# k transposed by pairs of tokens, C's exponentials by token parity, A in token order, one store per output tile, and a new order table

## The chip, the core and the metric

The kernel runs on one core of a Trainium2 chip. The metric is the time of one execution on the device in microseconds. Before the change it is 270.56 us, the median of three runs (270.55 to 273.65). A difference of 2% is 5.4 us.

The core has a matrix engine (TensorE, PE in the profile; its weight loads are PEld), a vector engine (VectorE, DVE), an activation engine (ScalarE, ACT), GpSimd (POOL) and SyncE (SP), which here only issues transfers. PSUM is the memory that PE writes; eight banks of 512 float32 columns on 128 partitions.

## The reference, cut to what matters

Eight batches, eight heads, 576 tokens of 64 elements. Tokens are averaged in 32 segments of 18 (the landmarks). Three softmax matrices are made, a small pseudo-inverse is iterated six times, and the attention's result goes through a two-layer MLP.

```python
q_lm = q.reshape(B, H, m, S // m, D).mean(axis=3)      # m = 32 landmarks
k_lm = k.reshape(B, H, m, S // m, D).mean(axis=3)
A  = sm(q, k_lm)        # 576 x 32 for each head
Bm = sm(q_lm, k_lm)     # 32 x 32
C  = sm(q_lm, k)        # 32 x 576
for _ in range(6):
    Z = 2 * Z - Z @ Bm @ Z
attn = A @ Z @ C @ v
x = attn.transpose(0, 2, 1, 3).reshape(B * S, H * D)   # 4608 x 512
h = x @ w_in                                           # 512 -> 2048
out = (max(h, 0) ** 2) @ w_out                         # 2048 -> 512
```

## The kernel before

**Layout.** A token of a segment r (0 to 31) is r*18 + t, with t from 0 to 17. The eight heads of a batch are two halves i of four groups g; a partition is g*32 + r. q and k are loaded by half (`kraw`, `qraw`), v in four quarters: block c of v's partitions holds tokens t = 9c to 9c + 8.

**Attention of a batch** (`attention`, L474). `tr` (L538 to 549) transposes q and k on PE, six blocks of 128x128 at a time; ACT or DVE evicts them to `qT` and `kT`. The text of `tr` has a branch for q, which transposes two neighbouring tokens at once (so that plane c of 64 partitions holds tokens 2j + c), and one for k, which would take 64-column halves. The function reads the loop's variable `nm` when the plan is emitted, and by then it is "q": the trace has L543 for k as for q, and no L548. Batch 0's landmark sums are made on PE (`l_sum`, L507), the others on DVE and POOL (`add9` to `add0`, L486). The small matrix B and the six iterations are a chain of short instructions (`Eb`, `BB`, `st`, `upd`: L579 to L670).

For C, `c_mm` (L683) multiplies the landmarks of q with kT: for each half eight matmuls of 288 columns, one for each group g and plane c, on eight separate 64x32 parts of the PE array. `nmc` (L688) takes the maximum on DVE, `c_exp` (L691) the exponentials on ACT with their sum, `c_tr` (L702) transposes them, `cv` (L718) multiplies with v in 72 small matmuls, `rcv` (L709) and `cv_ev` (L726) divide. In this kernel row (c, j) of the transposed C stands for k's token 2j + c and meets v's token 9c + j; in the changed kernel both are the same token.

For A, `a_mm` (L765), `a_t` (L774), `a_max`, `a_sub`, `a_exp`, `a_sum`, `a_rec`, `a_mul` and `a_xp` (L793) make `AT`: 32 rows per group over the batch's 576 tokens, in the order t*32 + r. `g_mm` (L804) makes G, the product of the small matrices, v and w_in, so that the first layer of the MLP is one product of G and AT.

**MLP of a batch.** `mlp_in` (L812): 16 blocks f of four matmuls of 288 columns (L823), a relu (ACT L840 or DVE L842) and a square (ACT L848 or DVE L850) to `gs`. `mlp_out` (L863): tiles of 128 tokens, for each 16 matmuls of 512 columns (L884), eviction (L301 on ACT, L303 on DVE) to one of five buffers `o`, and the stores. A tile's 128 rows are in the order t*32 + r, so `store` (L854) issues four transfers of 32 rows, 18 rows of the output apart. The last tile is cut in two halves of 256 columns, whose stores go to SP and ACT in turn.

**What sets the order.** Nothing is scheduled at run time. Every step is recorded as an operation of a plan; `ORDER` is a written-out table that gives, for each operation in turn, its number, its engine where there is a choice (relu, square, evictions, additions, masks), and its PSUM bank. A negative number puts filler matmuls of zeros (L445) there. `PACE` is a second table: an operation, most often one on POOL, waits for a named earlier one. Each engine works through its part of the table in order. So the attention of batch b + 1 and the MLP of batch b are interleaved by hand, and POOL's loads (L362, L368, L396, L404) start where the table puts them.

Of the kernel before, what the change touches and what calls it, by code (L numbers as in the profile page):

```python
# [8 lines left out]
P = 128  # L9
AF = mybir.ActivationFunctionType  # L10
ALU = mybir.AluOpType
AX = mybir.AxisListType
# [8 lines left out]
M = 32  # L21
# [247 lines left out]
def kernel(  # L269
# [35 lines left out]
    def scaled(e, dst, src, by):  # L305
        if e == "ACT":
            nc.scalar.activation(dst, src, AF.Copy, scale=by)
        else:
# [15 lines left out]
    Eb = sb.tile([P, 2, M], F32, name="Eb")  # L324
    BB = sb.tile([P, 2, M], F32, name="BB")
    sm = {nm: sb.tile([P, 2], F32, name=nm)
          for nm in ("nmb", "rs", "rr", "cs", "mx", "cc", "rc", "nmc", "rsc", "rcv")}
    BTc = sb.tile([P, 2, M], BF16, name="BTc")
    BTf = sb.tile([P, 2, M], F32, name="BTf")
    BTd = sb.tile([P, 2, NG, M], BF16, name="BTd")  # L330
# [621 lines left out]
```

## Time and profile before

| | us |
|---|---|
| median of three runs | 270.56 |
| profiled execution | 270.56 |
| its span | 268.8 |
| PE busy | 253.9 |
| DVE busy | 204.0 |
| ACT busy | 202.2 |
| POOL busy | 111.4 |
| first L823 matmul of batches 0, 1, 2 | 26.28, 54.17, 79.87 |
| last matmul ends | 263.5 |

The profile is of one execution. Busy time is the union of an engine's instructions; a group's row gives line, engine, operation, what is written and read, its shape, the count, the busy time, the mean duration of one in ns, and the idle time of the engine just before them with what ended it. A row of windows gives the busy time of each engine in a stretch (with the number of instructions in brackets), the granted PE clock, the share of the DMA engines and the bandwidth. A row of a timeline gives start, length and what it is; in square brackets stands the idle time before it. Matmuls are pipelined: a 512-column matmul (L884) is shown 373 ns long and the next starts 216 ns after it; a 288-column one (L823) 286 and 122.

### The profile page before, as it was taken

To read this page: it belongs to the slowest core of one execution; us is meant where nothing else is said; L and a number is where in the kernel's file an instruction comes from. 1 tells how busy PE (TensorE), PEld (TensorE's weight loads), DVE (VectorE), ACT (ScalarE), POOL (GpSimd) and SP (SyncE) were. 2 spreads that over 40 slices of the span, in tenths; PEclk is the share of its full clock that TensorE was granted. 3 is DMA by queue.
4 is the path that set the end of the run, shared out by engine and by line. 5 is a ranking of instruction groups with operands and counts; after the bars stand their busy time and mean duration, and the time that the engine had idled before them with its cause. 6 is when DMAs were issued, how large, how long until landed. Compare 5 with 4: busy or idle time off the path is not lost.

```text
span 268.8 us, 7634 instructions
## 1 busy us (share of the span) xinstructions
PE 253.9 (94%) x2969; PEld 155.5 (58%) x3005; DVE 204.0 (76%) x530; ACT 202.2 (75%) x385; POOL 111.4 (41%) x181
## 2 busy tenths in 40 slices
PE   8878899999999999999999999999999999999992
PEld 8656655557654655555655565555646655465551
DVE  1498989979987898798897689679898887945130
ACT  2755999999997879879988679876878857466500
POOL 8468648755344163526463444535410144100000
PEclk9999999999999999999999999999999999999998
DMA  6999999269518822596229806493303422022143
GB/s 151 204 206 207 208 198 177 37 96 209 142 22 124 187 45 70 61 163 130 45 61 165 130 29 133 56 220 56 74 7 78 82 71 52 0 68 51 39 119 77
DMA packets 20723, 28.57 MB, mean 106 GB/s; under 512 B 3536, under 2 KB 11984, under 8 KB 20688
## 3 DMA queue, kind: packets, MB, share of 16 engines
q0 software_dynamic: 13296, 18.06, 42.8%
q1 hardware_dynamic: 7200, 9.91, 13.3%
q8 instruction: 23, 0.38, 0.6%
q10 hardware_dynamic: 192, 0.13, 0.2%
q14 instruction: 12, 0.10, 0.1%
HBM read 36.70 MB, written 9.44 MB: 172 GB/s over the span
## 4 chain that ended last, share of the span: by engine, by line
PE 81%; DVE 6%; ACT 4%; issue 3%; DMA 3%; POOL 2%; DVEq 0%; POOLq 0%
PE ps L884 45%; PE ps L823 21%; PE ps L543 4%; PE ps L804 3%; DMA kraw<-in_k_dram 3%; PE ps L718 2%; PE ps L650 1%; PE ps L702 1%; ACT G L301 1%; PE ps L445 1%; PE ps L683 1%; DVE SA L774 1%; PE ps L765 1%; ACT r L840 1%; DVE mxA L777 1%
## 5 line engine op out<-in xcount | busy, mean ns | idle before, releaser
L884 PE MATMUL ps<-w_out_bf,gs 128*128 128x512 bf16 (+1 forms) x556 | 140.0, 373 | 2.5 <-issue 1.4
L823 PE MATMUL ps<-AT,G 128*128 128x288 bf16 x512 | 79.0, 286 | 0.9 <-DVE r L842 0.5
L884 PEld LDWEIGHTS <-gs 128*128 128x128 bf16 x592 | 54.0, 98 | 43.6 <-issue 4.7
L840 ACT ACTIVATE r<-ps 128x576 bf16<-128x576 f32 x95 | 60.3, 652 | 13.9 <-PE ps L823 10.1
L848 ACT ACTIVATE gs<-r 128x576 bf16<-128x576 bf16 x95 | 62.8, 682 | 8.7 <-DVE r L842 8.0
L823 PEld LDWEIGHTS <-G 128*128 128x128 bf16 x512 | 48.0, 98 | 22.1 <-issue 1.5
L842 DVE TENSOR_SCALAR r<-ps 128x576 bf16<-128x576 f32 x33 | 24.7, 752 | 11.6 <-PE ps L823 6.7
L368 POOL DMA_DIRECT2D vraw<-in_v_dram x32 | 18.1, 567 | 30.0 <-DVE EA L790 6.0
L301 ACT CAST G<-ps 128x512 bf16<-128x512 f32 x47 | 24.9, 598 | 4.2 <-PE ps L804 4.1
L303 DVE COPY o<-ps 128x512 f32<-128x512 f32 (+1 forms) x17 | 11.4, 670 | 10.3 <-PE ps L884 7.0
L301 ACT COPY o<-ps 128x512 f32<-128x512 f32 (+1 forms) x20 | 11.3, 572 | 10.3 <-PE ps L884 10.2
L790 POOL TENSOR_TENSOR EA<-EA,rA 128x576 bf16<-128x576 bf16 x12 | 13.8, 1154 | 9.9 <-DVE rA L788 5.3
L691 ACT ACTIVATE EC<-ps,nmc 128x576 bf16<-128x576 f32 x16 | 11.8, 738 | 7.2 <-DVE nmc L688 6.9
L850 DVE TENSOR_TENSOR gs<-r 128x576 bf16<-128x576 bf16 x33 | 14.8, 460 | 2.0 <-ACT r L840 1.9
L779 POOL TENSOR_TENSOR SA<-SA,mxA 128x576 f32<-128x576 f32 x12 | 13.9, 1158 | 3.8 <-DVE mxA L777 1.9
L660 DVE SCALAR_TENSOR_TENSOR st<-st,ps 128x128 bf16<-128x128 bf16 x40 | 11.1, 277 | 4.8 <-PE ps L650 3.5
L774 DVE STREAM_TRANSPOSE SA<-ps 128x576 f32<-128x576 f32 x16 | 12.2, 773 | 3.1 <-PE ps L765 2.8
L445 PE MATMUL ps<-zero 128*128 128x128 bf16 x147 | 11.6, 239 | 2.9 <-DVE st L660 1.4
L594 POOL TENSOR_TENSOR Pd<-st,ones_d 128x256 bf16<-128x256 bf16 x13 | 9.2, 707 | 11.8 <-DVE st L660 7.4
L543 PE MATMUL ps<-perm,qraw 128*128 128x128 bf16 x144 | 12.1, 219 | 0.7 <-DMA qraw<-in_q_dram 0.6
L793 DVE STREAM_TRANSPOSE AT<-EA 128x576 bf16<-128x576 bf16 x16 | 12.3, 767 | 0.4 <-POOL EA L790 0.2
L362 POOL DMA_DIRECT2D qraw<-in_q_dram x16 | 9.0, 562 | 8.4 <-DVE BTc L303 2.1
(126 smaller groups left out, 370.8 us busy)
## 6 DMA issues: line engine op xcount, KB each, us to landing
out_dram<-o SPq DMA_DIRECT2D x140, 64.0 KB, 2.0
qraw<-in_q_dram POOLq DMA_DIRECT2D x16, 288.0 KB, 5.7
vraw<-in_v_dram POOLq DMA_DIRECT2D x32, 144.0 KB, 4.1
kraw<-in_k_dram POOLq DMA_DIRECT2D x15, 288.0 KB, 5.4
w_in_bf<-in_moe_w_in_dram POOLq DMA_DIRECT2D x4, 512.0 KB, 8.7
w_out_bf<-in_moe_w_out_dram POOLq DMA_DIRECT2D x4, 512.0 KB, 8.8
gs<-in_k_dram SPq DMA_DIRECT2D x2, 288.0 KB, 4.3
out_dram<-o ACTq DMA_DIRECT2D x4, 32.0 KB, 1.7
```

The lines of the kernel that those rows point to most:

```text
L301: nc.scalar.copy(dst, src)
L368: nc.gpsimd.dma_start(vraws[z][p0:p0 + 32, :, :, :].rearrange("p g t d -> p g (t d)"), src[b].rearrange("(g i) (r t) d -> i r g (t d)", i= ...
L445: mm(ps[:, bank, 0:P], lhsT=zero[:], rhs=zero[:], start=True, stop=True)
L543: nc.tensor.transpose(t[:, x * P:(x + 1) * P], raw[:, i, 2 * j:2 * j + 2, :].rearrange("p t d -> p (t d)"), perm[:])
L774: add("a_t", "DVE", lambda e, sa=sa, i=i: nc.vector.transpose(SA[:, i, :, :].rearrange("p (c j) m -> p c (j m)", c=2), two(sa)[:, :, 0:HALF]),
L779: add("a_sub", "DVE POOL", lambda e, i=i, spread=spread: ENG[e].tensor_tensor(SA[:, i, :, :], SA[:, i, :, :], spread(mxA[:, i, :]), ALU.su ...
L823: mm(t[:, j, 0:HALF], lhsT=G[:, i, f * P:(f + 1) * P], rhs=AT[:, i, j * HALF:(j + 1) * HALF], start=(i == 0), stop=(i == 1))
L840: nc.scalar.activation(r.rearrange("p (j t) -> p j t", j=2), src, AF.Relu)
L842: nc.vector.tensor_scalar(out=r.rearrange("p (j t) -> p j t", j=2), in0=src, scalar1=0.0, scalar2=None, op0=ALU.max)
L848: nc.scalar.activation(dst, r[:], AF.Square)
L850: nc.vector.tensor_tensor(dst, r[:], r[:], ALU.mult)
L884: mm(one(ok)[:, 0:hi - lo], lhsT=gs[:, f, x0:x0 + P], rhs=w_out_bf[:, f, lo:hi], start=(f == f0), stop=(f == f1 - 1))
```

## The change

1. `tr` has only the pair branch, for k and q alike.
2. `c_mm` writes the odd plane in two pieces: tokens of j = 4 to 8 first (160 columns), then j = 0 to 3 (128 columns). Twelve matmuls for eight.
3. `c_exp` is two activations, one over the first five blocks of both planes, one over the last four with the planes swapped; each gives its own sum, and `rsum`, a new operation on DVE, adds the two. `cv` takes v's blocks in the order that fits.
4. `a_xp` writes AT in token order, r*18 + t: neighbours of the input go to columns 18 elements apart.
5. A tile's rows are then neighbours in the output, and `store` is one transfer of 128 rows (two for the last tile, one on SP and one on ACT).
6. ORDER and PACE are new throughout. By count of the tables: fillers 147 before, 165 after; relus on ACT 95 and 90 (of 128), squares on ACT 95 and 98, G evictions on ACT 47 and 42 (of 64), output evictions of 512 columns on ACT 19 and 21 (of 35), additions of the landmark sums on POOL 59 and 74 (of 140), paced operations 161 and 174. On POOL the first loads are, before: second half of k, both halves of q, then batch 1's; after: first half of q, second half of k, second half of q, then batch 1's k.

```diff
--- before
+++ after
@@ ORDER, PACE @@
-    592, 32, 280, 72, 472, 720, 160, 200, -551, 2180, 344, 2248, -63, 1605, 408, 1368, 1664, 1736, 2630, 2311, 2696,
...
+    592, 32, 72, 408, 280, 536, 656, 160, 344, 472, 720, 784, -583, 2884, 2952, 200, -111, 2181, -79, 1606, 1664,
...
@@ -325,6 +320,7 @@
     BB = sb.tile([P, 2, M], F32, name="BB")
     sm = {nm: sb.tile([P, 2], F32, name=nm)
           for nm in ("nmb", "rs", "rr", "cs", "mx", "cc", "rc", "nmc", "rsc", "rcv")}
+    rsc = sb.tile([P, 2, 2], F32, name="rscs")
     BTc = sb.tile([P, 2, M], BF16, name="BTc")
     BTf = sb.tile([P, 2, M], F32, name="BTf")
     BTd = sb.tile([P, 2, NG, M], BF16, name="BTd")
@@ -539,14 +535,9 @@
                     t = one(tp).bitcast(BF16)
                     for x in range(6):
                         i, j = divmod(6 * u + x, NJ)
-                        if nm == "q":
-                            nc.tensor.transpose(
-                                t[:, x * P:(x + 1) * P],
-                                raw[:, i, 2 * j:2 * j + 2, :].rearrange("p t d -> p (t d)"), perm[:])
-                            continue
-                        for c in range(2):
-                            nc.tensor.transpose(
-                                t[64 * c:64 * c + 64, x * P:(x + 1) * P], raw[:, i, NJ * c + j, :], perm[:])
+                        nc.tensor.transpose(
+                            t[:, x * P:(x + 1) * P],
+                            raw[:, i, 2 * j:2 * j + 2, :].rearrange("p t d -> p (t d)"), perm[:])
 
                 add("trk" if nm == "k" else "tr", "PE", tr,
                     reads=[y for i in sorted({6 * u // NJ, (6 * u + 5) // NJ}) for y in ready(nm, b, i)] + ["perm"], writes=[tp], acq=("n", tp))
@@ -680,19 +671,23 @@
                 t = two(sc)
                 for g in range(NG):
                     for c in range(2):
-                        mm(t[M * g:M * g + M, c, 0:HALF], lhsT=dups["q"][64 * c:64 * c + 64, i, g, :],
-                           rhs=Ts["k"][z][64 * c:64 * c + 64, NJ * i:NJ * i + NJ, g, :],
-                           start=True, stop=True)
+                        for lo, hi, at in ((0, NJ, 0),) if c == 0 else ((4, NJ, 0), (0, 4, 5)):
+                            mm(t[M * g:M * g + M, c, M * at:M * (at + hi - lo)],
+                               lhsT=dups["q"][64 * c:64 * c + 64, i, g, :],
+                               rhs=Ts["k"][z][64 * c:64 * c + 64, NJ * i + lo:NJ * i + hi, g, :],
+                               start=True, stop=True)
 
             add("c_mm", "PE", c_mm, reads=[("q", "dup")] + keyT["k"][i], writes=[sc], acq=("h", sc))
             add("nmc", "DVE", lambda e, sc=sc, i=i: nc.vector.tensor_reduce(
                 out=sm["nmc"][:, i:i + 1], in_=two(sc)[:, :, 0:HALF], axis=AX.XY, op=ALU.max, negate=True),
                 reads=[sc], writes=[("nmc", i)])
-            add("c_exp", "ACT", lambda e, sc=sc, i=i: nc.scalar.activation(
-                EC[:, :, i, :, :].rearrange("p j c r -> p c j r"),
-                two(sc)[:, :, 0:HALF].rearrange("p c (j r) -> p c j r", j=NJ),
-                AF.Exp, bias=sm["nmc"][:, i:i + 1], scale=1.0, accum_out=sm["rsc"][:, i:i + 1]),
-                reads=[sc, ("nmc", i)], writes=[("EC", z, i), ("rsc", i)])
+            for odd in range(2):
+                add("c_exp%d" % odd, "ACT", lambda e, sc=sc, i=i, odd=odd: nc.scalar.activation(
+                    (EC[:, 5:9, i, ::-1, :] if odd else EC[:, 0:5, i, :, :]).rearrange("p j c r -> p c j r"),
+                    two(sc)[:, :, 5 * M * odd:(5 + 4 * odd) * M].rearrange("p c (j r) -> p c j r", r=M),
+                    AF.Exp, bias=sm["nmc"][:, i:i + 1], scale=1.0,
+                    accum_out=rsc[:, i, odd:odd + 1]),
+                    reads=[sc, ("nmc", i)], writes=[("EC", z, i, odd), ("rsc", i, odd)])
         for u, (t0, n) in enumerate(((0, 5), (5, 4))):
             et = (A, "et", u)
 
@@ -702,12 +697,15 @@
                     nc.tensor.transpose(t[:, x * P:(x + 1) * P],
                                         EC[:, t0 + x, :, :, :].rearrange("p i c r -> p (i c r)"), ident[:])
 
-            add("c_tr%d" % n, "PE", c_tr, reads=[("EC", z, 0), ("EC", z, 1), "ident"], writes=[et], acq=("n", et))
+            add("c_tr%d" % n, "PE", c_tr, reads=[("EC", z, i, u) for i in range(2)] + ["ident"],
+                writes=[et], acq=("n", et))
             add("c_ev%d" % n, "DVE ACT", lambda e, et=et, t0=t0, n=n: copy(
                 e, ECT[:, t0:t0 + n, :].rearrange("p t x -> p (t x)"),
                 one(et).bitcast(BF16)[:, 0:n * P]), reads=[et], writes=[("ECT", z, u)])
+        add("rsum", "DVE", lambda e: nc.vector.reduce_sum(sm["rsc"][:], rsc[:], axis=AX.X),
+            reads=[("rsc", i, odd) for i in range(2) for odd in range(2)], writes=["rsum"])
         add("rcv", "DVE", lambda e: nc.vector.reciprocal(sm["rcv"][:], sm["rsc"][:]),
-            reads=[("rsc", 0), ("rsc", 1)], writes=["rcv"])
+            reads=["rsum"], writes=["rcv"])
         cv = (A, "cv")
 
         def cv_mm(e):
@@ -716,7 +714,7 @@
                 for g in range(NG):
                     for i in range(2):
                         mm(t[M * g:M * g + M, i, 0:D], lhsT=ECT[64 * i:64 * i + 64, x, M * g:M * g + M],
-                           rhs=vraws[z][64 * i:64 * i + 64, g, x, :], start=(x == 0), stop=(x == NJ - 1))
+                           rhs=vraws[z][64 * i:64 * i + 64, g, 2 * x if x < 5 else 2 * x - 9, :], start=(x == 0), stop=(x == NJ - 1))
 
         add("cv", "PE", cv_mm, reads=[("ECT", z, 0), ("ECT", z, 1)] + [("v", z, g) for g in range(NG)],
             writes=[cv], acq=("h", cv))
@@ -791,7 +789,7 @@
                 EA[:, i, :, :], EA[:, i, :, :], spread(rA[:, i, :]), ALU.mult),
                 reads=[("rA", i), ("EA", z, i)], writes=[("EN", z, i)])
             add("a_xp", "DVE", lambda e, i=i: nc.vector.transpose(
-                AT[:, i, :], EA[:, i, :, :].rearrange("p t m -> p (t m)")),
+                AT[:, i, :].rearrange("p (r t) -> p t r", t=SEG), EA[:, i, :, :]),
                 reads=[("EN", z, i), ("EA", z, i)], writes=[("AT", z, i)])
 
         for n in range(4):
@@ -851,24 +849,21 @@
 
             twin.append(add("square", "DVE ACT", square, reads=[("r", rn)], writes=wk))
 
-    def store(osb, key, pieces, lo=0, hi=DM):
-        for p0, b, x0, n in pieces:
-            to = out[b * S:(b + 1) * S, :].rearrange("(r t) n -> r t n", t=SEG)
-            for x in range(0, n, M):
-                def go(e, p=p0 + x, t=(x0 + x) // M, to=to):
-                    ENG[e].dma_start(to[:, t, lo:hi], osb[p:p + M, lo:hi])
-
-                add("store%d" % (M * (hi - lo) // 512), "SP ACT" if hi - lo < 512 else "SP", go, reads=[key])
+    def store(osb, key, row, lo=0, hi=DM):
+        def go(e):
+            ENG[e].dma_start(out[row:row + P, lo:hi], osb[:, lo:hi])
+
+        add("store%d" % (hi - lo), "SP ACT" if hi - lo < DM else "SP", go, reads=[key])
 
     def mlp_out(b):
         plan.batch = b
         z = b % 2
         if z == 0:
-            tiles = [("g", t * P, [(0, b, t * P, P)]) for t in range(4)]
+            tiles = [("g", t * P) for t in range(4)]
         else:
-            tiles = [("gx", DM, [(0, b - 1, DM, 64), (64, b, 0, 64)])]
-            tiles += [("g", S + 64 + t * P, [(0, b, 64 + t * P, P)]) for t in range(4)]
-        for t, (sk, x0, pieces) in enumerate(tiles):
+            tiles = [("gx", DM)] + [("g", S + 64 + t * P) for t in range(4)]
+        for t, (sk, x0) in enumerate(tiles):
+            row = (b - z) * S + x0
             parts2 = 2 if b == 0 else 1
             last = b == B - 1 and t == len(tiles) - 1
             on = state["o"] % NO
@@ -896,9 +891,9 @@
                         add("o_add", "DVE", lambda e, ok=ok, osb=osb: nc.vector.tensor_tensor(
                             osb[:], osb[:], one(ok), ALU.add), reads=[ok, ("ob", on, 0)], writes=[("ob", on, 0)])
                     if last:
-                        store(osb, ("ob", on, lo), pieces, lo, hi)
+                        store(osb, ("ob", on, lo), row, lo, hi)
             if not last:
-                store(osb, ("ob", on, 0), pieces)
+                store(osb, ("ob", on, 0), row)
 
```

303 rows, old and new, of tables (ORDER, PACE) are left out of this document.

## The prediction

> **What bounds the kernel now.** I read the page's busy times and chain first, then the windows by stage, then the groups by form, then the timelines of single places.
>
> ```profile
> PE 253.9 (94%) x2969; PEld 155.5 (58%) x3005; DVE 204.0 (76%) x530; ACT 202.2 (75%) x385; POOL 111.4 (41%) x181
> ...
> PE 81%; DVE 6%; ACT 4%; issue 3%; DMA 3%; POOL 2%; DVEq 0%; POOLq 0%
> ```
>
> TensorE carries 81% of the chain that ended last. But that is a mean over stages, so I cut the span at the first L823 matmul of a batch (26.28, 54.17, 79.87 us and so on) and at the last matmul (263.5):
>
> ```profile
> core 0: us, PE busy (x) PEld busy (x) DVE busy (x) ACT busy (x) POOL busy (x), PEclk, DMA share, GB/s
> 26.30:54.30 28.00, 26.09 (x338) 16.03 (x340) 25.62 (x70) 27.35 (x55) 18.91 (x34) 1.00 0.92 153
> 54.30:77.00 22.70, 22.44 (x280) 14.09 (x281) 20.64 (x62) 21.71 (x43) 11.24 (x18) 1.00 0.74 139
> 77.00:107.00 30.00, 29.25 (x338) 16.58 (x343) 24.63 (x69) 25.36 (x50) 11.93 (x20) 1.00 0.48 94
> ...
> 36.40:263.50 227.10, 223.51 (x2439) 131.77 (x2475) 180.08 (x460) 178.08 (x337) 87.37 (x137) 1.00 0.49 93
> ```
>
> The reader is to see three stages. Up to 26.3 us there is no main matmul: batch 0's attention is a chain of small DVE, ACT and PE steps. From 26.3 to 54.3 ACT is busy 27.35 of 28.00 us and is the bound. After that PE is: idle only 3.6 of 227.1 us from 36.4 on, so there whatever PE must do more is paid in full, and what DVE or ACT do more is paid only where PE runs out of matmuls. Behind the last matmul lie 5.3 us.
>
> **The change, part by part.** I work against the profiled execution: span 268.8 us and 1.76 us around it, 270.56, which is also the median of the three runs.
>
> *k by pairs of tokens: nothing.* The helper that transposes reads the loop's variable when the plan is emitted, so the old text already ran the pair branch for k:
>
> ```profile
> L543 PE MATMUL ps<-perm,kraw 128*128 128x128 bf16 x144 | 10.4, 220 | 0.0
> ...
> L683 PE MATMUL ps<-kT,qdup 64*32 64x288 bf16 x128 | 3.9, 288 | 0.0
> ...
> L691 ACT ACTIVATE EC<-ps,nmc 128x576 bf16<-128x576 f32 x16 | 11.8, 738 | 7.2 <-DVE nmc L688 6.9
> ...
> L793 DVE STREAM_TRANSPOSE AT<-EA 128x576 bf16<-128x576 bf16 x16 | 12.3, 767 | 0.4 <-POOL EA L790 0.2
> ```
>
> 144 is 18 a batch, as for q; the changed program has the same 144.
>
> *C's scores (L683), on PE.* Eight matmuls of 288 columns on eight separate 64x32 tiles of the array become twelve: for each group g, the odd plane is cut into 160 and 128 columns on the same tile. Now:
>
> ```profile
> 56.23 0.41 PE L804 MATMUL ps<-w_in_bf,WT 64*32 64x512 bf16 x8
> 56.46 0.30 PE L683 MATMUL ps<-kT,qdup 64*32 64x288 bf16 x8
> 56.58 0.22 PE L567 MATMUL ps<-kdup,qdup 64*32 64x32 bf16 x8
> ```
>
> Each eight starts when the eight before on the same tiles have streamed: 0.23 us behind 512 columns, 0.12 us behind 288, 0.42 ns a column. In the new order the second odd piece follows the first at once on its own tile, so it waits 160 x 0.42 = 0.07 us, and if the next group waits behind it, four times. First start to end of stream is then 4 x 0.07 + 128 x 0.42 = 0.33 us instead of 0.12 + 0.02: +0.20 us a time. If free tiles overtake, nothing is added, because each tile still streams 288 columns. I take 0.20, as every start that I looked at is in the program's order; ends 0 and 0.25. Fourteen of the sixteen stand behind 26.3 us: +2.8 us.
> The Trainium skill, page "TensorE: Matmul & The Clock Gate", section "The mechanism", says that matmuls start and end strictly in program order; by it the sum is the +2.8 taken, without it 0. The rows here agree with it, but none shows a free tile behind a blocked one.
>
> *C's exponentials (L691), on ACT.* One of 576 becomes 320 + 256, each with its read of the accumulator. From 32 elements (298 ns, the Eb group) to 576 (738) it is 0.81 ns an element and 272 fixed, so 531 + 479 against 738; from start to start the fixed part that can't overlap is about 0.25. +0.25 us a time, 4 us over 16. The new DVE sum of the two parts costs what the smallest DVE reductions cost, 0.21 us eight times; behind it the reciprocal and C·v's eviction wait, but C·v's 72 matmuls take 0.7 us beside it: nothing outside the start.
>
> *Stage 26.3 to 54.3, where ACT ends last.* Here the new table counts. From batch 0's first L823 group to batch 1's, the old table lists 48 ACT instructions, by their rows 30.7 us (27.35 us as a union, since neighbours overlap); the new one 52 and 32.3, with two more for the split, two more relus, one Eb and one BTc, against one G eviction and one WT fewer. +1.6 by rows, 1.6 x 27.35 / 30.7 = **+1.4 us**. PE's own +0.4 of C's scores lies beside that. Ends: 0, if PE has other matmuls listed; 3, if DVE (29.3 to 31.1 by rows) also lags.
>
> *Later stages, where PE ends last.* Twelve C scores, +2.4. By counts and start-to-start times (216 ns for L884, 122 for a L823) the new table lists 0.5 us less PE work behind batch 1's first group, having done it earlier. **+1.9**, ends -0.5 and +2.5. The switches between tiled and full matmuls are 110 against 109. POOL takes 8 us more by rows; with 111 of 269 us busy it hides it.
>
> *The start: -1.0.* Of batch 0's loads the order on POOL changes, not the bytes before q's second half, which lands at 9.86 us and is what the chain waits for. Old: q's transposes go before its landmark sums, and on DVE the addition khalf of batch 1, which waits for a load until 11.28, stands ahead of qls.
>
> ```profile
> 11.28 0.46 DVE L486 TENSOR_TENSOR khalf<-kraw 128x576 bf16<-128x576 bf16 x1 [0.36 <-DMA kraw<-in_k_dram]
> 11.65 0.42 DVE L309 TENSOR_SCALAR qls<-ps 128x256 bf16<-128x256 f32 x1
> ```
>
> In the new order the sums go first and khalf is on POOL: qls about 1.0 earlier. One a_max (0.75) moves from beside Eb onto the chain to the first st. In the iterations a kT copy (0.55), a khalf (0.44) and 14 filler matmuls in one place (0.78) go, and an ECT copy (0.42), the sum (0.2), two more groups of 8 fillers in the chain (net 0.1) and the longer exponentials (0.2) come. -1.0 + 0.75 - 1.77 + 0.92 = -1.1; I take -1.0, ends -2 and +0.8.
>
> *A in token order (L793), on DVE.* Same 16 instructions; the output goes to steps of 18 elements of two bytes. No row writes so. The nearest is the perm copy, which reads in steps of 4 elements: 227 ns against 228 for ones_d of the same size. I take 0; the upper end is twice the time, +0.77 each.
>
> *One store per tile; the end.* SP issues 37 stores for 144. While PE works they are free. At the end they are not:
>
> ```profile
> 263.53 0.37 ACT L301 COPY o<-ps 128x256 f32<-128x256 f32 x1 [8.09 <-PE ps L884]
> 263.94 0.85 ACTq L859 DMA_DIRECT2D out_dram<-o  x2
> 263.95 2.69 SPq L859 DMA_DIRECT2D out_dram<-o  x6
> ```
>
> SP's last issue starts at 266.23 and lands 1.56 later. After the change the last store is one issue on ACT at 263.94. It carries 128 KB, not 32; between 64 KB (1.70 to land) and 288 KB (3.25, the first k load) that is about 2.15, and a 256 KB store issued just before it on SP lands near 266.6. Against 267.78: **-1.2**, ends -1.7 and -0.3.
>
> Sum: 270.56 - 1.0 + 1.4 + 1.9 - 1.2 = **271.7 us**.
>
> **The rivals.**
> 1. *The four pieces of C's scores overlap.* Then the PE part falls from +1.9 to -0.5: 269.3. For: tiles are separate. Against: the ordered starts above. 0.13.
> 2. *The strided write doubles L793; slower.* Place: DVE, in the start, where both transposes stand in the last 3 us before the first L823 (24.03 and 25.46 us), +1.5; then 14 times 0.77, 10.8 us, against DVE idle of 2.4 of 28.0 and 5.4 of 30.0 us in the windows. If half is covered, +5.4: 278.6. It decides from about 0.5 us extra an instruction (1.0 + 3.5 = 4.5). Against: the perm row. 0.15. The Trainium skill, page "SBUF — State Buffer", section "Door 1: The DMA port swizzle", says that SBUF has lines of 16 bytes and each access to a new line pays; 36 bytes are a new line each time. By that rule this rival holds; no run here shows it yet.
> 3. *The new table leaves PE waiting.* It is another arrangement; if its waits behind 54 us are 5 us more than now (3.6 in 227), 276.7. For: ACT and DVE each have under 5 of 30 us to spare. 0.11.
> 4. *The new table mends the early stage; faster.* From 26.3 to 36.4 PE has matmuls for about 7.5 of 10.1 us. Without those 2.6 us and the +1.4, with a start 2 us shorter and rival 1's C: 271.7 - 2.6 - 1.4 - 1.0 - 2.4 = 264.3. 0.07.
> That the change does nothing in its first part is in the forecast.
>
> **How the numbers follow.** Forecast 0.54, then 0.13, 0.15, 0.11, 0.07. 2% is 5.4 us, about what a measurement of this kernel can tell from no change: 265.1 and 276.0. Faster 0.07. Slower: rivals 2 and 3 and the forecast's upper edge (strands of +2 to +3 in two parts at once), 0.27. Within 0.66. The range, 267.5 to 278.0, leaves out rival 4 and the worse half of rival 2; for the forecast alone it is 269 to 275.
>
> **What would show it.** First L823 at about 25.3 us; its batch 1 some 1.4 us later than 27.9 after it; L683's twelve over 0.33 us against 0.14; L793 at 767 ns; last landing about 3.1 us behind the last matmul, 4.3 now. I am wrong if L793 is over 1.2 us, if PE idles over 5 us behind 60 us, or if C's twelve take no longer.

## The result, and the profile after

The changed kernel takes 297.64 us, the median of four runs (296.77 to 298.80), against 272.11 of the kernel before on the same chip (four runs, 270.55 to 274.95). The ratio is 1.0962, with an interval of 1.0861 to 1.1064. It is **slower by 9.6%**; the forecast was 271.7, and the range ended at 278.0. The profiled execution of the changed kernel took 296.77 us, its span is 295.0.

The page of the changed kernel, busy times first, then the granted clock in 40 slices, then the chain that ended last, by engine and by line:

```profile
PE 263.4 (89%) x3047; PEld 161.2 (55%) x3087; DVE 231.3 (78%) x527; ACT 205.6 (70%) x414; POOL 118.2 (40%) x195
...
PEclk9998699979999999999997999979999999999999
...
PE 67%; DVE 22%; issue 5%; ACT 2%; DMA 2%; POOL 1%; DVEq 0%; POOLq 0%; ACTq 0%
PE ps L879 33%; PE ps L821 20%; DVE AT L791 11%; PE ps L538 4%; DVE G L298 3%; DMA kraw<-in_k_dram 2%; PE ps L697 1%; PE ps L716 1%; PE ps L802 1%; PE ps L763 1%; PE ps L641 1%; DVE sA L784 1%; PE ps L675 1%; ACT gs L846 1%; DVE SA L772 1%
```

DVE's share of the chain has gone from 6 to 22%, and half of that is one line, L791. That is the transpose `a_xp`, L793 before (lines have moved up by two to eight). DVE has three instructions fewer than before and 27.3 us more to do. The groups by form of the changed kernel show whose they are (count, then busy us and mean ns of one, then the idle time before them):

```profile
L821 PE MATMUL ps<-AT,G 128*128 128x288 bf16 x512 | 83.8, 295 | 15.2 <-DVE AT L791 7.8 <-DVE G L298 3.2 <-DVE ks L482 2.0
L791 DVE STREAM_TRANSPOSE AT<-EA 128x576 bf16<-128x576 bf16 x16 | 41.6, 2652 | 0.0
L538 PE MATMUL ps<-perm,kraw 128*128 128x128 bf16 x144 | 11.5, 223 | 0.2 <-DMA kraw<-in_k_dram 0.2
L685 ACT ACTIVATE EC<-ps,nmc 128x320 bf16<-128x320 f32 x16 | 8.5, 530 | 2.1 <-DVE nmc L681 2.0
L685 ACT ACTIVATE EC<-ps,nmc 128x256 bf16<-128x256 f32 x16 | 7.5, 475 | 1.9 <-DVE nmc L681 1.9
```

The same 16 instructions take 2652 ns instead of 767, so 16 x 1.885 = 30.2 us more. PE's first-layer matmuls, which read what this line writes, now wait 15.2 us where they waited 0.9. Their row in the kernel before:

```profile
L823 PE MATMUL ps<-AT,G 128*128 128x288 bf16 x512 | 79.0, 286 | 0.9 <-DVE r L842 0.5 <-ACT r L840 0.2
```

One of those places, at the start of batch 1's first layer, first DVE's timeline and then PE's (start, length, what; idle time before it in square brackets):

```profile
55.23 2.65 DVE L791 STREAM_TRANSPOSE AT<-EA 128x576 bf16<-128x576 bf16 x1
57.54 0.86 DVE L298 CAST G<-ps 128x512 bf16<-128x512 f32 x1
58.33 0.52 DVE L298 COPY kT<-ps 128x768 bf16<-128x768 bf16 x1
58.79 2.61 DVE L791 STREAM_TRANSPOSE AT<-EA 128x576 bf16<-128x576 bf16 x1
```

```profile
59.06 0.61 PE L879 MATMUL ps<-w_out_bf,gs 128*128 128x512 bf16 x2
61.46 0.85 PE L821 MATMUL ps<-AT,G 128*128 128x288 bf16 x4 [1.79 <-DVE nmb L570]
```

The second transpose ends at 61.40 and the matmuls that read it begin at 61.46. The bracket names L570 because that short reduction is shown to end at the same time; the L821 matmuls don't read it. Ahead of the same place PE had also waited 0.95 us for the G eviction that stands between the two transposes.

The windows of the changed kernel, cut at the first L821 matmul of a batch, the last row from batch 0's to the last matmul:

```profile
core 0: us, PE busy (x) PEld busy (x) DVE busy (x) ACT busy (x) POOL busy (x), PEclk, DMA share, GB/s
27.40:61.40 34.00, 28.74 (x360) 18.31 (x361) 31.49 (x85) 28.59 (x59) 15.62 (x27) 0.90 0.83 126
61.40:91.50 30.10, 28.30 (x312) 16.60 (x318) 26.27 (x59) 24.64 (x49) 14.24 (x24) 0.94 0.53 100
91.50:124.20 32.70, 29.42 (x347) 16.77 (x350) 28.98 (x64) 25.99 (x53) 18.68 (x32) 1.00 0.42 83
27.40:291.80 264.40, 241.27 (x2587) 142.65 (x2624) 215.97 (x488) 191.07 (x381) 97.92 (x161) 0.97 0.44 86
```

PE is idle 23.1 of 264.4 us. In the first window DVE is the fullest engine, 31.49 of 34.00 us. The granted clock is 0.90 and 0.94 in two of the windows: in or right behind the waits PE was granted half speed for 3.4 or 6.8 us at a time, 17 us in all. Whether that costs anything of its own is asked below.

The end is shorter. The last matmul ends at 291.82 and the span 3.2 us later, against 5.3 before:

```profile
290.97 0.40 SPq L854 DMA_DIRECT2D out_dram<-o  x1
...
291.86 0.37 ACT L296 COPY o<-ps 128x256 f32<-128x256 f32 x1 [1.38 <-PE ps L879]
292.26 0.38 ACTq L854 DMA_DIRECT2D out_dram<-o  x1
```

### The profile page after: what moved, and what is told of

Read it like the earlier page. It is cut to its first block, busy times and chain, and to the rows that moved or that the text cites. A ratio compares the mean times of both kernels' runs of the same rounds, so it can differ in the third digit from the quotient of the medians.

```text
span 295.0 us, 7686 instructions
## 1 busy us (share of the span) xinstructions
PE 263.4 (89%) x3047; PEld 161.2 (55%) x3087; DVE 231.3 (78%) x527; ACT 205.6 (70%) x414; POOL 118.2 (40%) x195
## 4 chain that ended last, share of the span: by engine, by line
PE 67%; DVE 22%; issue 5%; ACT 2%; DMA 2%; POOL 1%; DVEq 0%; POOLq 0%; ACTq 0%
PE ps L879 33%; PE ps L821 20%; DVE AT L791 11%; PE ps L538 4%; DVE G L298 3%; DMA kraw<-in_k_dram 2%; PE ps L697 1%; PE ps L716 1%; PE ps L802 1%; PE ps L763 1%; PE ps L641 1%; DVE sA L784 1%; PE ps L675 1%; ACT gs L846 1%; DVE SA L772 1%
## 5 line engine op out<-in xcount | busy, mean ns | idle before, releaser
L821 PE MATMUL ps<-AT,G 128*128 128x288 bf16 x512 | 83.8, 295 | 15.2 <-DVE AT L791 7.8
L838 ACT ACTIVATE r<-ps 128x576 bf16<-128x576 f32 x90 | 57.5, 652 | 33.1 <-PE ps L821 23.4
L821 PEld LDWEIGHTS <-G 128*128 128x128 bf16 x512 | 49.1, 100 | 39.8 <-issue 12.8
L791 DVE STREAM_TRANSPOSE AT<-EA 128x576 bf16<-128x576 bf16 x16 | 41.6, 2652 | 0.0
L840 DVE TENSOR_SCALAR r<-ps 128x576 bf16<-128x576 f32 x38 | 28.5, 752 | 12.8 <-PE ps L821 9.4
L296 ACT CAST G<-ps 128x512 bf16<-128x512 f32 x42 | 22.8, 591 | 13.5 <-PE ps L802 13.2
L685 ACT ACTIVATE EC<-ps,nmc 128x256 bf16<-128x256 f32 (+1 forms) x32 | 15.6, 502 | 4.0 <-DVE nmc L681 3.8
L298 DVE CAST G<-ps 128x512 bf16<-128x512 f32 x22 | 16.0, 744 | 1.7 <-PE ps L802 1.5
L298 DVE COPY o<-ps 128x512 f32<-128x512 f32 x14 | 9.5, 683 | 9.0 <-PE ps L879 9.0
L802 PE MATMUL ps<-w_in_bf,WT 64*32 64x512 bf16 x256 | 11.4, 390 | 5.2 <-DVE G L298 3.8
L296 ACT COPY qT<-ps 128x768 bf16<-128x768 bf16 x13 | 10.4, 801 | 5.4 <-PE ps L538 5.3
L358 POOL DMA_DIRECT2D kraw<-in_k_dram x15 | 8.4, 560 | 12.5 <-DVE BTf L580 4.6
```

Of the source, the lines that this page charges most:

```text
L296: nc.scalar.copy(dst, src)
L298: ENG[e].tensor_copy(dst, src)
L685: add("c_exp%d" % odd, "ACT", lambda e, sc=sc, i=i, odd=odd: nc.scalar.activation((EC[:, 5:9, i, ::-1, :] if odd else EC[:, 0:5, i, :, :]) ...
L791: add("a_xp", "DVE", lambda e, i=i: nc.vector.transpose(AT[:, i, :].rearrange("p (r t) -> p t r", t=SEG), EA[:, i, :, :]), reads=[("EN", z ...
L821: mm(t[:, j, 0:HALF], lhsT=G[:, i, f * P:(f + 1) * P], rhs=AT[:, i, j * HALF:(j + 1) * HALF], start=(i == 0), stop=(i == 1))
L838: nc.scalar.activation(r.rearrange("p (j t) -> p j t", j=2), src, AF.Relu)
```

## The experiments

The theory was that the **stepped write** makes L791 long and that this is the whole loss. Its rivals were that the new table is to blame, and that the half clock behind the waits is a loss of its own.

### Contiguous transposes in the changed kernel

```diff
-                AT[:, i, :].rearrange("p (r t) -> p t r", t=SEG), EA[:, i, :, :]),
+                AT[:, i, :], EA[:, i, :, :].rearrange("p t m -> p (t m)")),
```

> The changed kernel with one edit undone: the 16 transposes that make AT write in the order t*32 + r again, without steps between neighbours. The stores stay one per tile, so the output's rows are left in that order. Theory S (the stepped write, 2652 ns against 767, makes the whole loss through DVE): the transposes are back at 770 ns, no wait of PE over 1.5 us before a batch's first main matmul, granted clock over 0.99, and 268 to 272 us. Rival T (the new table leaves PE waiting by itself): the transposes are short too, but the time stays over 280 us with waits at the batches' starts.

Measured: 267.13 us (266.81 to 267.78), ratio to the kernel before 0.9858, interval 0.9814 to 0.9903. The page's busy times and the L821 group of this kernel:

```profile
PE 255.4 (96%) x3047; PEld 159.3 (60%) x3087; DVE 203.4 (77%) x527; ACT 204.5 (77%) x414; POOL 117.9 (44%) x195
...
L821 PE MATMUL ps<-AT,G 128*128 128x288 bf16 x512 | 79.6, 286 | 0.5 <-DVE SA L772 0.2
```

Its windows, cut in the same way:

```profile
26.30:53.30 27.00, 26.06 (x362) 16.92 (x364) 26.49 (x85) 26.81 (x57) 15.90 (x29) 1.00 1.01 164
53.30:80.40 27.10, 26.64 (x313) 16.24 (x317) 24.12 (x62) 25.77 (x52) 14.70 (x26) 1.00 0.61 117
26.30:262.40 236.10, 232.18 (x2588) 139.20 (x2625) 190.09 (x488) 190.08 (x381) 98.08 (x163) 1.00 0.50 98
```

A transpose takes 759 ns again. With the same table and the same instructions PE is idle 3.9 of 236.1 us instead of 23.1 of 264.4, and the clock is full. The time lies 0.9 us below the range that was expected. The stepped write is worth 297.64 - 267.13 = 30.5 us by the medians and 29.4 us by the profiled spans (295.0 and 265.6), and the new table is not to blame. By batch, from one first L821 to the next, the changed kernel is longer by 7.1, 2.9, 3.5, 3.5, 2.4, 5.0 and 3.9 us, and not at all in the last stage, where no transposes are left; 1.0 us comes in the start. That is 29.4 us against the 30.2 that DVE got more to do. So next to nothing of it was hidden, unless the half clock added what was hidden; that is taken up below.

### The stepped write alone, in the kernel before

```diff
-                AT[:, i, :], EA[:, i, :, :].rearrange("p t m -> p (t m)")),
+                AT[:, i, :].rearrange("p (r t) -> p t r", t=SEG), EA[:, i, :, :]),
```

> The kernel before with one edit: its 16 transposes write AT in steps of 18 elements, as in the changed kernel; the stores stay as they were, so the output's rows are left in another order. S: 2650 ns each, 30 us more on DVE, and as the old table has no more room for it than the new one, 288 to 302 us. T: DVE's idle time in the old table takes most of it, under 280 us.

Measured: 302.34 us, ratio 1.1163 (1.1087 to 1.1239). The group of this kernel:

```profile
L793 DVE STREAM_TRANSPOSE AT<-EA 128x576 bf16<-128x576 bf16 x16 | 42.2, 2638 | 0.4 <-POOL EA L790 0.2
```

The time is just above the 288 to 302 us expected. The duration is that of the changed kernel and the loss, 31.6 us against 270.79 on that chip, is about the same, with the old table and without any other part of the change. Put together with the run before, the cause of the loss is shown from both sides.

### The half clock

Forty filler matmuls before the first L821 of each batch, in the changed kernel:

```diff
+            if op.tag == "in_mm" and op.turn == 0:
+                self.fill(code % 8, 40)
+                n = len(traced())
             op.fn(e)
```

> The changed kernel with 40 filler matmuls (2.2 us at full clock) ahead of each batch's first main matmul, where PE waits 2 to 3 us for AT. The result is the same. Theory H (part of the loss is the granted clock, at half for 17 us in four stretches behind those waits, 8.5 us of PE time): the half-clock stretches go, and the time falls by 3 to 8 us, to 290 to 294 us. Rival: the waits alone count, the time behind them would be lost anyway to DVE: 296 to 300 us.

Measured: 299.44 us, ratio 1.1042 (1.0975 to 1.1109). The mean clock rises from 0.969 to 0.987, and only two stretches of half clock are left (3.4 us each, from 27.0 and 156.7); the time doesn't fall. The 3 to 8 us that the theory promised did not come. But this doesn't show that the half clock costs nothing, because the fillers cost time themselves. In batch 4 they begin at 157.49, behind the same wait and at half clock, and the first L821 stands at 160.96 where it stood at 156.75. In batch 5 it begins 1.5 us behind the end of the first transpose (193.26 and 191.75), where it began 0.06 behind it (189.24 and 189.18).

In two places where the half clock went, from 61.8 and from 191.5, the time from the end of the batch's second transpose to that of the next batch's fell: 29.33 us for 30.64, and 36.11 for 37.60. The next stage behind the first of them grew by 1.7 us. So the fillers' cost and what the clock gave back can't be told apart here, and a loss of some 1.5 us a stretch stays possible. It would be part of what the stepped write costs: with contiguous transposes the waits and the half clock both are gone.

### What a step costs

Each batch's transposes with another distance between neighbours, k elements of two bytes:

```diff
-                AT[:, i, :].rearrange("p (r t) -> p t r", t=SEG), EA[:, i, :, :]),
+                AT[:, i, :].rearrange("p (a r k) -> p a k r", r=M, k=(1, 18, 2, 3, 6, 9, 18, 1)[b]),
+                EA[:, i, :, :].rearrange("p (a k) m -> p a k m", k=(1, 18, 2, 3, 6, 9, 18, 1)[b])),
```

> The changed kernel with another step of AT's transposes in each batch: neighbours go 1, 18, 2, 3, 6, 9, 18 and 1 elements of two bytes apart for batches 0 to 7 (the order of the tokens in the output is left out). Theory L (each new line of 16 bytes is paid for): 2 and 3 elements, 4 and 6 bytes, stay near 770 ns, 6 elements (12 bytes, mostly a new line) are between, 9 and 18 (18 and 36 bytes) both take about 2650. Rival P (any write that is not to the neighbour is paid for): every batch but the first and the last is at 2650. Rival B (the price grows with the bytes spanned): 9 is at about half of 18.

DVE's timeline of this kernel, one row for steps of 1, 18, 2, 3, 6 and 9 elements; the rows with x2 hold two transposes:

```profile
23.76 0.72 DVE L791 STREAM_TRANSPOSE AT<-EA 128x576 bf16<-128x576 bf16 x1
...
50.04 2.65 DVE L791 STREAM_TRANSPOSE AT<-EA 128x576 bf16<-128x576 bf16 x1
...
81.53 0.83 DVE L791 STREAM_TRANSPOSE AT<-EA 128x576 bf16<-128x576 bf16 x1
...
111.95 1.15 DVE L791 STREAM_TRANSPOSE AT<-EA 128x576 bf16<-128x576 bf16 x1
...
141.02 4.04 DVE L791 STREAM_TRANSPOSE AT<-EA 128x576 bf16<-128x576 bf16 x2
...
175.43 5.23 DVE L791 STREAM_TRANSPOSE AT<-EA 128x576 bf16<-128x576 bf16 x2
```

| step, elements (bytes) | the two of the batch, us | 16-byte lines entered, of 576 writes | 4.4 ns a line + 0.13 |
|---|---|---|---|
| 1 (2) | 0.72, 0.78 | 72 | 0.45 |
| 2 (4) | 0.83, 0.84 | 144 | 0.76 |
| 3 (6) | 1.15, 1.12 | 216 | 1.08 |
| 6 (12) | 2.12, 2.20 | 432 | 2.03 |
| 9 (18) | 2.72, 2.88 | 576 | 2.66 |
| 18 (36) | 2.65, 2.61 | 576 | 2.66 |

The rows fit a price that goes by how often the write enters a new 16-byte stretch of a partition: a step of 36 bytes costs no more than one of 18, where every write already enters a new stretch. (At step 1 something else limits, some 1.25 ns an element.) The 4.4 ns and the 0.13 us are fitted to these rows, and the two transposes at step 9 are up to 0.22 us longer. The two rivals expected for this run, a price for every write that isn't to the neighbour and one that grows with the bytes spanned, don't give the rise from 6 to 12 to 18 bytes with the flat end behind it. Theory L missed in one place: at 6 bytes it expected about 770 ns. Only the rows are used of this run; it was timed once, at 283.16 us.

The Trainium skill, page "SBUF — State Buffer", section "Door 1: The DMA port swizzle", has the line of 16 bytes and says that each access to a new one pays; the rows agree. It also says that two hits a line are enough for full bandwidth, and that one can stride 8 bf16 elements for free. For these writes the measurement differs and decides: a step of 3 elements, with 2.7 hits a line, already takes 1.13 us against 0.75, and one of 6 elements 2.16.

### Token order on PE's side

Transposes contiguous, and PE's moving operand read in token order instead, in steps of 32 elements (64 bytes):

```diff
-                        mm(t[:, j, 0:HALF], lhsT=G[:, i, f * P:(f + 1) * P],
-                           rhs=AT[:, i, j * HALF:(j + 1) * HALF], start=(i == 0), stop=(i == 1))
+                        mm(t[:, j, 0:HALF].rearrange("p (r t) -> p r t", t=SEG), lhsT=G[:, i, f * P:(f + 1) * P],
+                           rhs=AT[:, i, :].rearrange("p (t r) -> p r t", r=M)[:, 16 * j:16 * j + 16, :],
+                           start=(i == 0), stop=(i == 1))
```

> The changed kernel, AT written without steps, and the token order made where PE reads AT: the main matmuls' moving operand has 16 runs of 18 columns, 64 bytes from one column to the next. The whole computation stands. If PE's reads do not pay for the step: L821 stays at 122 ns from start to start and the time is that of the kernel whose transposes alone are undone, 268 to 272 us. If a new 16-byte line costs a read as it seems to cost DVE's writes (2.65/0.77 = 3.4 times): 290 ns more for each of 512 matmuls, over 400 us; half of that is still over 330 us.

Measured: 489.74 us, ratio 1.8041 (1.7931 to 1.8152). The group of this kernel:

```profile
L821 PE MATMUL ps<-AT,G 128*128 128x288 bf16 x512 | 264.1, 659 | 0.9 <-DVE G L298 0.6 <-issue 0.2
```

From start to start, at full clock, an L821 matmul now takes 484 ns against 122: 1.68 ns a column for 0.42. The step costs PE four times the time, 512 times over: 512 x 0.362 = 185 of the 222.6 us between this kernel and the one with contiguous transposes. The clock was half for 135 us of this run; in those stretches too an L821 took 484 ns, while other matmuls took longer (L880 427 ns from start to start for 216), which may be the rest and was not taken apart. Of the two places DVE's sixteen writes are the cheap one; neither is worth it here.

### What the one store per tile is worth

Contiguous transposes, and each tile stored in four transfers of 32 rows as before:

```diff
-            ENG[e].dma_start(out[row:row + P, lo:hi], osb[:, lo:hi])
+            for x in range(0, P, M):
+                b, x0 = divmod(row + x, S)
+                to = out[b * S:(b + 1) * S, :].rearrange("(r t) n -> r t n", t=SEG)
+                ENG[e].dma_start(to[:, x0 // M, lo:hi], osb[x:x + M, lo:hi])
```

> The changed kernel with AT written without steps and each tile stored by four transfers of 32 rows again, in the one place where the new table has its store: the whole computation in the right order, by the new table, without the step. If one store per tile is worth what the end says: against the kernel whose transposes alone are undone (267.1 us) the last transfers are four issues of 0.42 us in a row, so 1.0 to 1.5 us more, 268.1 to 268.6 us. If stores also delay buffers in the middle: over 270 us.

Measured: 271.28 us, ratio 1.0016 (0.9987 to 1.0044). The last matmul ends at 261.98, no later than with one store (262.40), but the span ends 7.8 us behind it instead of 3.2. The two ends, first of the kernel with one store a tile, then of this one (its lines stand three lower):

```profile
262.43 0.37 ACT L296 COPY o<-ps 128x256 f32<-128x256 f32 x1 [1.38 <-PE ps L879]
262.83 0.38 ACTq L854 DMA_DIRECT2D out_dram<-o  x1
```

```profile
261.38 6.07 SPq L857 DMA_DIRECT2D out_dram<-o  x11
...
262.01 0.37 ACT L296 COPY o<-ps 128x256 f32<-128x256 f32 x1 [1.37 <-PE ps L882]
262.42 1.80 ACTq L857 DMA_DIRECT2D out_dram<-o  x4
```

From 261.38 on SP still has eleven transfers to issue, the last one ends at 267.44 and lands at 268.74. They stand about 0.47 us apart, and there is one gap of 1.1 us, from 263.22 to 264.30: the transfer behind it waits for a semaphore that it shares with ACT's of 262.42, and that one lands at 264.28. With one store a tile SP's last issue ends at 261.95. A transfer of 128 rows takes about as long to issue (0.33 to 0.41 us) as one of 32 (0.31 to 0.46). So one store per tile is worth 271.28 - 267.13 = some 4.1 us in this table (the two were timed on different chips), all of it behind the last matmul. Expected were 1.0 to 1.5 us from ACT's four issues in a row; what was overlooked is SP's row, which ends last. The time over 270 us was expected for stores that delay the middle, and that is not what happened.

The next kernels kept the four transfers but dealt them out. The first gives the last tile's pieces to SP and ACT in turn:

```diff
-                ENG[e].dma_start(to[:, x0 // M, lo:hi], osb[x:x + M, lo:hi])
+                by = e if hi - lo == DM else ("SP", "ACT")[x // M % 2]
+                ENG[by].dma_start(to[:, x0 // M, lo:hi], osb[x:x + M, lo:hi])
```

> The same with the four transfers of the last tile's two halves given to SP and ACT in turn. Two issues less stand behind the last eviction on ACT: 0.8 us less if ACT's queue ends last, nothing if SP's, which stores the tile before in four pieces, does: 267.4 to 268.4 us.

Measured: 270.98 us, ratio 0.9997 (0.9972 to 1.0022). That is above the 267.4 to 268.4 us expected. SP still issues until 266.73, because four pieces of a full tile stand in its row ahead of its last two. So the next one deals out the last batch's last four tiles:

```diff
-                by = e if hi - lo == DM else ("SP", "ACT")[x // M % 2]
+                by = e if row < (B - 1) * S + 64 else ("SP", "ACT")[x // M % 2]
```

> AT without steps, four transfers of 32 rows for each tile, and those of the last batch's last four tiles given to SP and ACT in turn. The whole computation in the right order. If the whole gain of one store per tile lies in the queue of issues at the end (5.9 us of issues in a row on SP when ACT takes only half of the very last tile), the last landing moves to about 2.5 us behind the last matmul, and 267 to 268.5 us follow. If ACT's issues delay its own last evictions: 269 to 271 us.

Measured: **269.65 us** (268.97 to 270.79), ratio 0.9916 (0.9876 to 0.9955). It has the lowest median of the kernels that do all of the work, 0.8% below the kernel before, which is less than the 2% that counts as a change, and 9.4% below the changed one. Its end:

```profile
261.62 3.65 SPq L858 DMA_DIRECT2D out_dram<-o  x8
...
262.52 0.37 ACT L296 COPY o<-ps 128x256 f32<-128x256 f32 x1 [0.92 <-PE ps L883]
262.92 0.89 ACTq L858 DMA_DIRECT2D out_dram<-o  x2
```

From 261.4 on SP has eight issues for eleven, without the gap; they end at 265.27 and the span at 267.46. ACT's last eviction does begin late, at 262.52, behind ACT's own issues of 261.63 to 262.48, as the second case of the expectation had it; but SP's row still ends last. The last one puts POOL in ACT's place for the full tiles:

```diff
-                by = e if row < (B - 1) * S + 64 else ("SP", "ACT")[x // M % 2]
+                by = e if row < (B - 1) * S + 64 else ("SP", "ACT" if hi - lo < DM else "POOL")[x // M % 2]
```

> The same with POOL, idle by then, in ACT's place for the tiles before the last. ACT is free for its evictions; if a transfer issued by POOL lands as soon as one of SP (1.7 us), 267 to 268.5 us; if it needs the 4 us of POOL's loads, its last pair, issued about 1 us before the end of the matmuls, lands near the end all the same, 267.5 to 270 us.

Measured: 269.94 us, ratio 0.9923 (0.9894 to 0.9951). The intervals of the two overlap; nothing tells them apart. SP's row ends last here as well, its last issue at 266.21.

### C's part alone, in the kernel before

The twelve score matmuls, the two exponentials and the sum, with the old table:

```diff
+                        for lo, hi, at in ((0, NJ, 0),) if c == 0 else ((4, NJ, 0), (0, 4, 5)):
...
+            def c_exp(e, sc=sc, i=i):
+                for odd in range(2):
+                    nc.scalar.activation(
...
+        def rcv(e):
+            nc.vector.reduce_sum(sm["rsc"][:], rscs[:], axis=AX.X)
+            nc.vector.reciprocal(sm["rcv"][:], sm["rsc"][:])
```

> The kernel before with C's part of the change alone: twelve score matmuls for eight, two exponentials for one in the same places of the old table, the sum added on DVE just ahead of the reciprocal, v's blocks in the new order. By the prediction: 0.20 us for each of 14 score groups on PE and 0.25 us for each exponential in the stage that ACT bounds, 2.8 and up to 0.5 us, 273.5 to 274.5 us. By the changed kernel's trace, where twelve take as long as eight: PE pays nothing, 270.5 to 271.8 us.

Measured: 272.82 us, ratio 1.0065 (1.0032 to 1.0098), so +0.9 to +2.7 us. That lies between the two times expected, and the cost isn't where it was put. Where a batch's two sets of scores stand together, it is 386 ns from their first start to PE's next operation with 24 matmuls, against 372 with 16: 0.1 us over all batches. The rest comes in pieces of 0.1 to 0.4 us in most of the batches; which of the longer exponentials, the second accumulator read or the sum makes them was not taken apart.

## Why the prediction was wrong, by its steps

**The step that failed is "A in token order: I take 0".** The row it was read from, the perm copy, steps over 4 elements on a read. That is 8 bytes, two elements in every 16, so it never shows what one element in every 16 costs, let alone on a write. The row of the same size that it was compared with, ones_d, reads float32, so equal times didn't show either that the step was free. The upper end, twice the time, was a guess without a row, and +0.77 was far below the +1.885 measured. With no row near 36 bytes the open end should have been much wider, and rival 2's chance of 0.15 higher.

**Rival 2** had the place, the engine and the rule, and missed in two sizes. The first is the price: 2.65 us, not 1.53. The second is its "half is covered": with the price right it would still have said 271.7 + 3.8 + 13.2 = 288.7. The idle 5.4 of 30.0 us that it counted on as cover was spread over a DVE whose order is fixed. (Its windows end at 77 and 107 us, not at the first L823 of batches 2 and 3 as the text before them has it; between those, 79.87 and 111.02, DVE is idle 5.9 of 31.15 us, so little hangs on it.) The two transposes stand right before the matmuls that read them, and what lies between them (a G eviction, a kT copy) is late as well. In the changed kernel the window from 91.5 still shows DVE idle for 3.7 of 32.7 us, and PE for 3.3.

**The rest of the forecast** can be read from the kernel with contiguous transposes, whose profiled execution is 3.2 us below that of before, where the sum said +1.1. Its 267.13 us lies just below the range of 267.5 to 278.0:

| step | predicted, us | measured, us |
|---|---|---|
| start, to the first L821 | -1.0 | +0.06 |
| batch 0's stage | +1.4 | -0.95 |
| batch 1's first L821 to the last matmul | +1.9 | -0.2 |
| behind the last matmul | -1.2 | -2.1 |

- *k by pairs: nothing.* Right: L538 has 144 for k, as before.
- *The start.* The term that failed is `qls`, 1.0 earlier: it stands at 11.26 to 12.02 us in the nine kernels with the new table and at 11.59 to 12.01 in the three with the old one. The other two came. From `qls` to the first `st` it is 4.92 us in the contiguous kernel for 4.15 (+0.77, forecast +0.75), and from there to the first L821 9.40 for 10.48 (-1.08, forecast -0.85).
- *Batch 0's stage.* The sum of ACT's rows doesn't give the stage. The new table has 57 ACT instructions in the window for 55 and ACT is busy 26.81 us for 27.35; the sign was wrong. Which rows overlap more was not taken apart.
- *C's scores: +0.20 each.* Measured 0.015 us for a batch's two sets where they stand together, 386 to 388 ns for 371 to 372. Rival 1 was right: the 128-column pieces, third in the program's order of each group, start 82 to 118 ns in, while the next groups' 288- and 160-column ones start at 10 to 38 ns. A matmul on a free tile overtakes one that waits for its own tile. In the groups by form the 288-column ones are as long as before (288 ns):

```profile
L675 PE MATMUL ps<-kT,qdup 64*32 64x288 bf16 x64 | 3.7, 287 | 0.3
L675 PE MATMUL ps<-kT,qdup 64*32 64x160 bf16 x64 | 3.3, 235 | 0.0
L675 PE MATMUL ps<-kT,qdup 64*32 64x128 bf16 x64 | 3.1, 216 | 0.0
```

  The Trainium skill, page "TensorE: Matmul & The Clock Gate", section "The mechanism", has matmuls start and end strictly in program order; these starts differ, and the measurement decides. Without this term the later stages would have been forecast at -0.5; measured -0.2.
- *The exponentials.* 530 and 475 ns, forecast 531 and 479. The sum of two parts took 139 ns, not 0.21 us.
- *The end.* The mechanism was right, its size too small: -2.1, beyond its own end of -1.7. The last store lands 1.76 us after its issue, not 2.15, and SP's of 256 KB lands ahead of it, 2.19 after its issue at 261.54. Against four transfers with the same table it is 4.6, since SP would have eleven transfers left there (the old table left six behind 263.95) and one of them waits 1.1 us for a landing.
- *Rivals 3 and 4.* PE idles 3.9 us of 236 with contiguous transposes, so the new table leaves no waits (rival 3 falls). It does mend part of the early stage: 267.13 lies between rival 4's 264.3 and the forecast.

Of the signs named, L793 over 1.2 us and PE idle over 5 us behind 60 us both came (2.65 us, and 19.3 of 231.8 us), and both had the one cause. C's twelve took hardly longer either, which was the third.

## What to carry to other kernels

Before an operand's order is changed to spare transfers, count how many 16-byte stretches of a partition the new access pattern enters, and price it: here about 4.4 ns for each on a DVE write. On a PE read only one step was measured, 64 bytes, with 1.68 ns a column for 0.42. Where no row of the trace has a step that wide, one kernel with several steps in it answers what no neighbouring row can. And idle time of an engine in a written-out order need not be cover; here it was next to none: ask what reads the longer instruction and what stands between the two.

## What the runs showed of the hardware that was not expected

- A DVE transpose of 128x576 bf16 goes from 0.72 to 0.78 us (contiguous) to 2.61 to 2.88 us once neighbours are 18 bytes or more apart, and is flat from there.
- PE reading its moving operand in steps of 64 bytes streams at a quarter of its speed (484 ns for 122), at full and at half granted clock alike.
- Matmuls on free 64x32 tiles overtake a blocked one: 24 pieces take 386 ns, 16 matmuls of the same columns 372.
- A transfer that shares its semaphore with another engine's waits for that one's landing: 1.1 us on SP at the end of the kernel with four transfers a tile.
- In or right behind waits of PE of 1.8 to 3.0 us the granted clock was 0.5 for 3.4 or 6.8 us, four times; behind one of 2.8 us (121.5 to 124.3) it was not.
